# First group of a chunked recurrence: both scans first, score copies behind the packs, the turn behind those alone, 32 zero products ahead of the first T product

## The chip, the cores and the metric

One Trainium2 chip; the kernel runs on 1 core. The metric is the device time in microseconds of one execution. Engines: TensorE (PE, with its weight loads PEld), VectorE (DVE), ScalarE (ACT), GpSimd (POOL), SyncE (SP), and 16 DMA engines. Each engine works through its own instructions in the order in which they were put, and waits where an operand isn't ready. The order is made once, when the kernel is built: the program says what hangs on what, and a scheduler places the rest. Time before: 885.09 us, the median of three runs (878.41 to 887.28).

## What is computed

A recurrence over 768 steps for 4 x 8 heads with a 40 x 40 state, and behind it a layer of eight experts:

```python
for t in range(S):
    y[:, :, t] = np.einsum('bhd,bhde->bhe', rt, state)
    Sa = np.einsum('bhde,bhe->bhd', state, at)
    state_decay = state * wt[:, :, None, :] - np.einsum('bhd,bhe->bhde', Sa, bt)
    state = state_decay + np.einsum('bhd,bhe->bhde', vt, kt)
...
top2 = np.argpartition(-noisy_logits, 2, axis=1)[:, :2]
for e in range(E):
    for k in range(2):
        mask = top2[:, k] == e
        h = np.maximum(x[mask] @ w1[e], 0.0)
        out[mask] += top2_w[mask, k, None] * (h @ w2[e])
```

N is 3072 tokens, D 320, F 1024. The change lies in the recurrence alone.

## The kernel before

The 768 steps are cut into 12 chunks of 64 for each of two batch pairs p; `run` goes through the 24 chunks n = 0 to 23, p changing fastest. Two chunks of both pairs, four n, make a group g; there are six groups. For each group and pair some preparation is done ahead of its chunks:

- `prepA(G,raw)`: a scan over the decays w (the running product, `Gx`), its logarithm and the exponential of the negative on ACT (the inverse), three products for `NH` (a refined and shifted inverse) and `NG_`, then b times `NH` and a times `NG_`. `pack1` then splits b and a into a high and a low fp16 part: the high is a cast on ACT, the low a product on DVE, both in a buffer `pk` of which there are three (`PKB`). Three transfers for each, `st_ab<-pk`, stack them for PE: two need the high part alone, one the low.
- `prepC`: k times `NH`, packed as well, through DRAM (`d_k`) into `st_k`.
- `scoresL`: the score products `psc` of b and a for each chunk c, evicted from PSUM by DVE into `X` (the part for the solve) and by ACT into `lo`. PSUM has one buffer for them (`PPB`), so the products of the next chunk wait for both.
- `prepT`: `turn` transposes `X`, then `tsolve` inverts all 32 x 32 triangles in 30 steps of a product and an addition each; for group 0 on DVE, for the others on POOL (`TPOOL`). `prepU` turns `X` back: T is ready.

A chunk n is `pre` (the product `ak`, W), `chain` (T times W, twice, with a copy on ACT each time; the new state), `outp` and `blocks`. `warm(src,k)` issues k products of zeros into a PSUM tile that is overwritten later; `ND[0]` is 2.

The order around the change is set by the program's own sequence, by `V.run(z,at)`, which puts a preparation's DVE instructions behind the instruction `at` (a `Behind` object adds that edge and no wait), by `issue_after`, and for the rest by the scheduler. In `run`, the two preparations of group 0 stand one after the other, the score products are told to come behind the last cast `s.pa`, group 1's first preparation runs up to its b and a products with the k product of pair 1, and the turn of group 0 is put behind that k product by an edge of its own (`mk` behind `kl`). SP issues all transfers of this part.

## Time and profile before

| what | value |
|---|---|
| time, median of three | 885.09 us (878.41 to 887.28) |
| profiled execution | 874.69 us, of which the span 872.9 us |
| PE busy | 724.7 us (83%) |
| DVE busy | 593.7 us (68%) |
| ACT busy | 377.6 us (43%) |
| POOL busy | 366.1 us (42%) |
| DMA | 121.09 MB, mean 139 GB/s |

The span runs from the first to the last instruction; 1.8 us lie around it. Busy shares are means over stages that differ: the recurrence takes about the first half, the experts the second, and the work of this change lies in the first 100 us or so. What an edit is worth there is read from the waits and the order of time in that stretch, not from the table.

### The profile page before, as it was taken

Reading aid. Unit: us, or ns where it says so; the run is one execution under the profiler, and the core shown is the slowest. Engines: PE = TensorE matmul, PEld = TensorE weight load, DVE = VectorE, ACT = ScalarE, POOL = GpSimd, SP = SyncE. Lnnn points to the kernel's source line nnn. Section 1 sums busy time; section 2 is a strip of 40 time slices with the busy share of each in tenths; the row PEclk is TensorE's granted clock in tenths of the full one; section 3 lists DMA queues with packets and bytes.
Section 4 is the critical chain, followed back from the end, with each engine's and each line's share of the span. In section 5 each row is a group of like instructions: output and inputs, shape, how many; then the busy total and the mean of one; then the engine's idle time right before and its main releaser. Section 6 shows DMA issues by size and latency. Waiting matters only on the chain.

```text
span 872.9 us, 32590 instructions
## 1 busy us (share of the span) xinstructions
PE 724.7 (83%) x14248; PEld 647.4 (74%) x14248; DVE 593.7 (68%) x1305; ACT 377.6 (43%) x780; POOL 366.1 (42%) x512
## 2 busy tenths in 40 slices
PE   0124875899879787988998789999999999999993
PEld 0124664777767666777787688999999999999993
DVE  7799866887898897667667846828273746565530
ACT  3214444456555453544455525434343534444420
POOL 7000297495495396085002044344343434252222
PEclk9999889799999998999999999999999999999998
DMA  7766666477676284552223726594848585756312
GB/s 189 200 151 162 184 168 169 116 188 184 178 206 184 89 213 139 154 181 67 84 83 105 234 43 115 133 150 133 148 134 142 140 138 141 137 141 123 47 21 34
DMA packets 99508, 121.09 MB, mean 139 GB/s; under 512 B 37832, under 2 KB 83596, under 8 KB 99276
## 3 DMA queue, kind: packets, MB, share of 16 engines
q1 hardware_dynamic: 89244, 101.87, 45.3%
q0 software_dynamic: 10112, 17.05, 11.3%
q8 instruction: 113, 1.85, 0.9%
q14 instruction: 39, 0.32, 0.1%
HBM read 76.69 MB, written 24.74 MB: 116 GB/s over the span
## 4 chain that ended last, share of the span: by engine, by line
PE 62%; DVE 21%; POOL 5%; issue 4%; DMA 4%; ACT 3%; SPq 1%; POOLq 0%; DVEq 0%; ACTq 0%
PE ph L323 21%; PE po L350 18%; PE pW L563 4%; PE psc L563 4%; PE pY L563 3%; POOL X L686 3%; POOL Tt L684 2%; PE pQ L563 2%; DMA st_ab<-pk 2%; DVE pk L461 2%; PE pS L563 1%; DVE NH L461 1%; PE pst L563 1%; DVE P L807 1%; DVE X L461 1%
## 5 line engine op out<-in xcount | busy, mean ns | idle before, releaser
L353 POOL DMA_INDIRECT out_dram<-y,oi x56 | 87.5, 1563 | 188.0 <-ACT y L352 160.5
L323 PE MATMUL ph<-xT,w1h 128*128 128x256 f16 (+1 forms) x1280 | 137.3, 253 | 3.7 <-DVE xT L297 2.9
L323 PEld LDWEIGHTS <-w1h 128*128 128x128 f16 x1280 | 108.5, 98 | 12.3 <-issue 4.0
L350 PEld LDWEIGHTS <-hh 128*128 128x128 f16 x1536 | 107.9, 98 | 3.0 <-issue 3.0
L686 POOL TENSOR_TENSOR X<-X,Tt 128x30 f32<-128x30 f32 (+9 forms) x150 | 102.7, 685 | 11.1
L325 ACT ACTIVATE r<-ph 128x320 f32<-128x320 f32 (+1 forms) x128 | 65.3, 515 | 78.7 <-PE ph L323 63.5
L684 POOL TENSOR_TENSOR Tt<-X 128x30 f32<-128x30 f32 (+9 forms) x150 | 93.9, 626 | 10.7
L323 PE MATMUL ph<-xT,w1l 128*128 128x256 f16 (+1 forms) x768 | 89.4, 253 | 0.0
L261 DVE SCALAR_TENSOR_TENSOR w2l<-w2r,w2h 128x1280 f16<-128x1280 f32 x16 | 23.3, 1490 | 85.1 <-ACT w2h L260 85.1
L329 DVE TENSOR_TENSOR hl<-r,hh 128x256 f16<-128x256 f32 (+1 forms) x128 | 71.9, 562 | 4.0
L279 POOL DMA_INDIRECT xr<-xd,gi x56 | 57.4, 1025 | 34.5 <-ACT r L325 20.3
L679 POOL MEMSET X<- 128x32 f32 x5 | 0.8, 156 | 165.5 <-DVE X L676 165.5
L323 PEld LDWEIGHTS <-w1l 128*128 128x128 f16 x768 | 66.0, 98 | 4.4
L563 PEld LDWEIGHTS <-st_ab 120*32 120x32 f16 (+2 forms) x1312 | 26.7, 110 | 50.1 <-issue 47.7
L350 PE MATMUL po<-w2h,hh 128*128 128x160 f16 x768 | 61.1, 233 | 0.5 <-DVE f L153 0.5
L350 PE MATMUL po<-w2h,hl 128*128 128x160 f16 x768 | 61.0, 233 | 0.0
L350 PE MATMUL po<-w2l,hh 128*128 128x160 f16 x768 | 61.0, 233 | 0.0
L327 DVE CAST hh<-r 128x320 f16<-128x320 f32 (+1 forms) x128 | 49.1, 386 | 15.9 <-ACT r L325 15.6
L352 ACT ACTIVATE y<-po,tab 128x320 f32<-128x320 f32 x44 | 22.9, 521 | 77.9 <-PE po L350 77.9
L563 PE MATMUL psc<-RV,uT 128*64 128x128 f32 x384 | 54.3, 286 | 2.6 <-DVE P L807 2.4
L563 PE MATMUL pQ<-w,X 32*32 32x40 f32 x2304 | 39.6, 204 | 19.9 <-DVE X L676 7.5
L563 PEld LDWEIGHTS pQ<-w,X 32*32 32x32 f32 x2304 | 33.3, 111 | 29.8 <-issue 16.2
(352 smaller groups left out, 1601.9 us busy)
## 6 DMA issues: line engine op xcount, KB each, us to landing
st_ab<-pk SPq DMA_DIRECT2D x72, 180.0 KB
w2r<-in_w_dram SPq DMA_DIRECT2D x8, 1280.0 KB
RV<-in_rv_dram SPq DMA_DIRECT2D x48, 192.0 KB
w1r<-in_w_dram SPq DMA_DIRECT2D x8, 1024.0 KB
rawba<-in_fm_dram SPq DMA_DIRECT2D x20, 360.0 KB
raww<-in_fm_dram SPq DMA_DIRECT2D x12, 365.6 KB
d_k<-pk SPq DMA_DIRECT2D x12, 360.0 KB
st_k<-d_k SPq DMA_DIRECT2D x24, 180.0 KB
```

The costliest lines, as they stand in the source:

```text
L261: nc.vector.scalar_tensor_tensor(l,w,sc,o,op0=ALU.mult,op1=ALU.subtract,accum_out=s.wsum[:,s.nw:s.nw+1]); s.nw+=1
L279: k=t//128; s.held(nc.gpsimd.indirect_dma_start(out=X[:p,k if s.cap==CAP else 0],out_offset=None,in_=s.xd[int(w is not s.early[0])],in_off ...
L323: for a,b in cut(n): nc.tensor.matmul(ph[:,a:b],w[:,k,fs],X[:,j,t0+a:t0+b],start=i+a==0,stop=i==7,skip_group_check=True)
L325: g=nc.scalar.activation(r[:,:n],ph[:,:n],AF.Relu,scale=HSC/(XS*W1S))
L327: nc.vector.tensor_copy(hh[:,f,:n],r[:,:n])
L329: if c.stop>c.start: nc.vector.tensor_tensor(o,r[:,c],hh[:,f,c],op=ALU.subtract)
L350: for a,b in cut(DM): s.lm=nc.tensor.matmul(po[:p,a:b],h[:,f,r],w[:,f,a:b],start=k+a==0,stop=k==23,skip_group_check=True)
L353: st=nc.gpsimd.indirect_dma_start(out=s.out_d,out_offset=OFFS(ap=idx[:p,e,ii:ii+1],axis=0),in_=y[:p],in_offset=None,compute_op=ALU.add)
L461: i=f(*a,**k)
L563: def mm(s,*a,**k): return lambda: s.nc.tensor.matmul(*a,**k)
L684: eng.tensor_tensor(t,Xt[:,j:j+1,j+1:].to_broadcast([128,j,m]),Xt[:,0:j,j:j+1].to_broadcast([128,j,m]),op=ALU.mult)
L686: s.tl=eng.tensor_tensor(Xt[:,0:j,j+1:],Xt[:,0:j,j+1:],t,op=ALU.add)
```

## The change

`run` loads both decays ahead of everything else (`loadW`), and takes one step of each preparation in turn, so that both scans stand first; the second scan writes into a buffer of `st_ab` (`s3`), since `Gx` has one. The last pack's transfers are issued by ACT (`q`) and not by SP. DVE's copies of the first pair's scores are put behind the last low part (`pd`); the turn behind that alone, with its edge behind the k product gone; the k product of pair 1 behind step 20 of the solve (`tm0`). Chunk 0 gets 32 products of zeros (`NWU`) and not 2.

```diff
-NOUT=3072+896
+NOUT=3072+896; NWU=32
...
+    def loadW(s,p,g):
+        w=s.inp.tile([120,NS*65],F32,name="raww",bufs=2); s.nc.sync.dma_start(w,s.aps[0][p,g][:,:NS*65])
+        return w
-    def loadA(s,p,g,z=None):
+    def loadA(s,p,g,z=None,w=None):
...
-        w=s.inp.tile([120,W0],F32,name="raww",bufs=2); nc.sync.dma_start(w,FM[p,g][:,:W0])
+        if w is None: w=s.loadW(p,g)
...
-    def prepA(s,G,raw):
+    def prepA(s,G,raw,Gx=None,q=None):
...
-        Gx=s.tmp.tile([120,NS,65],F32,name="Gx")
+        if Gx is None: Gx=s.tmp.tile([120,NS,65],F32,name="Gx")
...
-        def stack(x):
+        def stack(x,e=nc.sync):
             def f(pk):
-                for q,l in ((40,0),(80,1),(0,x)): s.sd0=nc.sync.dma_start(sv[q:q+40,:,x],pk[:,l])
+                for q,l in ((40,0),(80,1),(0,x)): s.sd0=e.dma_start(sv[q:q+40,:,x],pk[:,l])
...
-        la=s.pack1(a_,-SC,0,1,stack(0))
+        la=s.pack1(a_,-SC,0,1,stack(0,q or nc.sync))
...
-    def scoresL(s,G,gi,scr):
+    def scoresL(s,G,gi,scr,f=None):
-        nc=s.nc
+        nc=s.nc; V=Behind(s.tc,nc.vector,f) if f is not None else nc.vector
...
-            s.sx=nc.vector.scalar_tensor_tensor(scr[:,q:q+8],pp[:,:,0:32],-(2.0**-18),s.tri.to_broadcast([128,8,32]),op0=ALU.mult,op1=ALU.mult)
+            s.sx=V.scalar_tensor_tensor(scr[:,q:q+8],pp[:,:,0:32],-(2.0**-18),s.tri.to_broadcast([128,8,32]),op0=ALU.mult,op1=ALU.mult)
...
-            s.warm(U,ND[0])
+            s.warm(U,ND[0] if o['n'] else NWU)
...
-        rA[0,0]=s.loadA(0,0)
+        w0=s.loadW(0,0); w1=s.loadW(1,0)
+        rA[0,0]=s.loadA(0,0,None,w0)
...
-        rA[0,1]=s.loadA(1,0,[xb(),xb()]); rC[0,0]=s.loadC({'p':0,'g':0})
+        rA[0,1]=s.loadA(1,0,[xb(),xb()],w1); rC[0,0]=s.loadC({'p':0,'g':0})
         s.consts1()
-        V.run(s.prepA(G_(0,0),rA[0,0])); rA[1,0]=s.loadA(0,1); V.run(s.prepA(G_(0,1),rA[0,1])); sd,pd=s.sd0.ins,s.pd
+        s3=s.sab[3].tile([120,18*K],F16,name="st_ab").bitcast(F32)[:,0:NS*65].rearrange("p (a b)->p a b",a=NS)
+        A=s.prepA(G_(0,0),rA[0,0]); B=s.prepA(G_(0,1),rA[0,1],s3,nc.scalar)
+        next(A); next(B); V.run(A); rA[1,0]=s.loadA(0,1); sd=s.sd0.ins; V.run(B); pd=s.pd
...
-            for p in range(2): scores(0,p)
+            for p in range(2): scores(0,p,None if p else pd)
...
-        prepT(0,s.pd); mk=s.xd; tl0=s.tl; tm0=s.tm
+        prepT(0,s.pd); tl0=s.tl; tm0=s.tm
...
-        for _ in range(5): next(z)
-        V.at=s.pl; c=s.prepC(grp[0][1],k1); next(c); kl=s.kl; V.at=tm0; next(c)
+        for _ in range(3): next(z)
+        V.run(s.prepC(grp[0][1],k1),tm0)
+        V.at=f1; next(z); next(z)
...
-        s.tc.add_manual_dep(mk.ins,kl.ins.name,mybir.DependencyInfo(mybir.DependencyClass.NoSync,mybir.DependencyReason.DATA),reason="behind")
```

The order on DVE at the start of the program, from the first scan on: `Gx` or, in the change, `st_ab` takes the scan, `raww` holds the inverse, `rawba` is b and a of pair 0. Before:

```order
L593 SCALAR_TENSOR_TENSOR Gx<-raww,d_111 120x780
L600 TENSOR_TENSOR NH<-Gx,raww 120x768
L603 SCALAR_TENSOR_TENSOR raww<-NH,raww 120x768
L605 TENSOR_TENSOR NH<-raww,Gx 120x768
L608 TENSOR_TENSOR NG__210<-Gx,raww 120x768
L613 TENSOR_TENSOR nge_212<-Gx,raww 120x12
L626 TENSOR_TENSOR rawba<-rawba,NH 120x768
L629 TENSOR_TENSOR rawba<-rawba,NG__210 120x768
L616 TENSOR_TENSOR gm<-nge_212,Gx 120x2x3x2
L553 SCALAR_TENSOR_TENSOR pk<-rawba,pk 120x768
L593 SCALAR_TENSOR_TENSOR Gx<-raww,d_111 120x780
L553 SCALAR_TENSOR_TENSOR pk<-rawba,pk 120x768
```

And in the change:

```order
L596 SCALAR_TENSOR_TENSOR Gx<-raww,d_111 120x780
L596 SCALAR_TENSOR_TENSOR st_ab<-raww,d_111 120x780
L603 TENSOR_TENSOR NH<-Gx,raww 120x768
L603 TENSOR_TENSOR NH<-st_ab,raww 120x768
L606 SCALAR_TENSOR_TENSOR raww<-NH,raww 120x768 x2
L608 TENSOR_TENSOR NH<-raww,Gx 120x768
L611 TENSOR_TENSOR NG__214<-Gx,raww 120x768
L616 TENSOR_TENSOR nge_216<-Gx,raww 120x12
L608 TENSOR_TENSOR NH<-raww,st_ab 120x768
L611 TENSOR_TENSOR NG__245<-st_ab,raww 120x768
L616 TENSOR_TENSOR nge_247<-st_ab,raww 120x12
L629 TENSOR_TENSOR rawba<-rawba,NH 120x768
```

Both scans now stand first, the two preparations alternate, and the low parts (`pk`) come behind all the products of both pairs.

The order on ACT in the same place, with buffer numbers and what each instruction waits for (DMAHW are the counters of transfers): lines 596/599 and 597/600 are the logarithm and the exponential, `pk` the casts, in the order b, a of pair 0, b, a of pair 1. Before:

```order
L596 ACTIVATE raww_177<-Gx_202 120x768 [waits DMAHW0_49,DVE_49]
L597 ACTIVATE raww_177<-raww_177 120x768 [waits Activation_49]
L551 ACTIVATE pk_219<-rawba_179 120x768 [waits DVE_49]
L551 ACTIVATE pk_222<-rawba_179 120x768 [waits DVE_49]
L596 ACTIVATE raww_184<-Gx_237 120x768 [waits DMAHW3_49,DVE_49]
L597 ACTIVATE raww_184<-raww_184 120x768 [waits Activation_49]
L551 ACTIVATE pk_254<-X_182 120x768 [waits DVE_49]
L551 ACTIVATE pk_257<-X_183 120x768 [waits DMAHW1_49,DMAHW2_49,DMAHW0_49,DVE_49]
```

And in the change:

```order
L599 ACTIVATE raww_177<-Gx_203 120x768 [waits DMAHW0_49,DVE_49]
L599 ACTIVATE raww_179<-st_ab_201 120x768 [waits DMAHW1_49,DVE_49]
L600 ACTIVATE raww_177<-raww_177 120x768 [waits Activation_49]
L600 ACTIVATE raww_179<-raww_179 120x768 [waits Activation_49]
L551 ACTIVATE pk_223<-rawba_181 120x768 [waits DVE_49]
L551 ACTIVATE pk_226<-rawba_181 120x768 [waits DVE_49]
L551 ACTIVATE pk_254<-X_184 120x768 [waits DVE_49]
L551 ACTIVATE pk_257<-X_185 120x768 [waits DMAHW1_49,DMAHW5_49,DMAHW0_49,DVE_49]
L626 DMA st_ab_252<-pk_257 40x3x768 [waits DMAHW2_49,Activation_49]
L626 DMA st_ab_252<-pk_257 40x3x768 [waits DMAHW4_49]
L626 DMA st_ab_252<-pk_257 40x3x768 [waits DMAHW6_49,DVE_49]
L673 ACTIVATE lo_269<-psc_270 128x256 [waits DVE_49]
```

Both logarithms stand ahead of both exponentials, and behind the fourth cast ACT issues that pack's three transfers, with the eviction and k's cast behind them. The fourth cast waits for three transfers of earlier packs in both orders.

The order on DVE around the second turn (`X<-X` of 32x32, group 1's), where chunk 0 ends and chunk 1 runs: `ak` belongs to `pre` of chunk 2, `uT` to the output of chunk 1, `rawk` is k of group 1's second pair. Before, from the copy `vu` on:

```order
L785 TENSOR_SCALAR vu<-pQ 64x320
L671 SCALAR_TENSOR_TENSOR X<-psc,tri 128x256
L102 SCALAR_TENSOR_TENSOR xT<-px,xT 128x384
L794 SCALAR_TENSOR_TENSOR Sst_162<-pS,gam_138 128x8x40
L461 TENSOR_TENSOR rawba<-rawba,NG__977 120x768
L671 SCALAR_TENSOR_TENSOR X<-psc,tri 128x256
L750 TENSOR_TENSOR sfs<-Sst_162,sfs 128x320
L676 STREAM_TRANSPOSE X<-X 128x32x32
L725 TENSOR_TENSOR ak<-psc,mk_123 128x512
L461 SCALAR_TENSOR_TENSOR pk<-rawba,pk 120x768
L567 COPY uT<-pu 128x512
L461 SCALAR_TENSOR_TENSOR pk<-rawba,pk 120x768
```

And in the change, from the state of chunk 1 on:

```order
L797 SCALAR_TENSOR_TENSOR Sst_162<-pS,gam_138 128x8x40
L461 TENSOR_TENSOR rawba<-rawba,NG__1007 120x768
L728 TENSOR_TENSOR ak<-psc,mk_123 128x512
L461 SCALAR_TENSOR_TENSOR pk<-rawba,pk 120x768
L753 TENSOR_TENSOR sfs<-Sst_162,sfs 128x320
L674 SCALAR_TENSOR_TENSOR X<-psc,tri 128x256
L102 SCALAR_TENSOR_TENSOR xT<-px,xT 128x384
L567 COPY uT<-pu 128x512
L461 SCALAR_TENSOR_TENSOR pk<-rawba,pk 120x768
L461 TENSOR_TENSOR rawk<-rawk,NH 120x6x64 x2
L674 SCALAR_TENSOR_TENSOR X<-psc,tri 128x256
L679 STREAM_TRANSPOSE X<-X 128x32x32
```

`ak`, two low parts (`pk`), `uT` and the k products (`rawk`, two instructions) stood behind the turn and now stand ahead of it. POOL's order is the same in both, and PE's differs in the first four chunks.

## Rows read from the trace of the kernel before

**Rows 1.** Waits, 135 to 175 us; columns: who for whom, us in total, times, longest

```profile
PE pQ L563 <- DVE X L461: 5.4, 1, 5.4
DVE X L461 <- POOL X L686: 4.6, 1, 4.6
```

**Rows 2.** Timeline, POOL, start of group 1's solve; columns: start us, us, instruction, [idle before]

```profile
104.08 0.15 POOL L679 MEMSET X<- 128x32 f32 x1 [85.55 <-DVE X L676]
```

**Rows 3.** Waits of DVE in the first 69 us

```profile
DVE X L671 <- PE psc L563: 5.4, 2, 3.4
DVE NH L600 <- ACT raww L597: 2.7, 2, 1.8
DVE pk L461 <- ACT pk L551: 0.5, 1, 0.5
```

**Rows 4.** Timeline, DVE, the first pair's preparation

```profile
4.90 1.78 DVE L593 TENSOR_TENSOR_SCAN Gx<-raww,d 120x780 f32<-120x780 f32 x1 [1.01 <-DMA raww<-in_fm_dram]
8.47 0.96 DVE L600 TENSOR_TENSOR NH<-Gx,raww 120x768 f32<-120x768 f32 x1 [1.78 <-ACT raww L597]
9.46 0.96 DVE L603 SCALAR_TENSOR_TENSOR raww<-NH,raww 120x768 f32<-120x768 f32 x1
12.40 0.95 DVE L626 TENSOR_TENSOR rawba<-rawba,NH 120x768 f32<-120x768 f32 x1
13.27 0.97 DVE L629 TENSOR_TENSOR rawba<-rawba,NG__210 120x768 f32<-120x768 f32 x1
```

**Rows 5.** Timeline, SP's queue; then the chain of work, start us, us, what

```profile
14.25 5.18 SPq L623 DMA_DIRECT2D st_ab<-pk  x6
...
18.68 5.00 DMA st_ab<-pk
65.02 2.44 DMA st_k<-d_k
```

**Rows 6.** Timeline, PE; sums of two windows: PE, PEld, DVE, ACT, POOL busy (instructions), PEclk, ...

```profile
61.03 0.71 PE L710 MATMUL pQ<-dm,idh 128*128 128x320 f16 x2
61.54 0.47 PE L563 MATMUL pS<-dm,idh 128*128 128x320 f16 x1
...
69.54 1.29 PE L563 MATMUL pQ<-w,X 32*32 32x40 f32 x64 [7.53 <-DVE X L676]
...
90.46 0.79 PE L563 MATMUL pQ<-w,X 32*32 32x40 f32 x64
...
69.50:70.80 1.30, 1.26 (x64) 1.16 (x64) 1.30 (x2) 0.56 (x1) 0.00 (x0) 1.00 0.05 13
151.80:153.20 1.40, 1.34 (x65) 1.25 (x65) 1.40 (x4) 0.00 (x0) 0.00 (x0) 0.50 0.14 38
```

**Rows 7.** Timeline, DVE and then POOL behind the second turn, and POOL at the solve's end

```profile
103.84 0.66 DVE L725 TENSOR_TENSOR ak<-psc,mk 128x512 f32<-128x512 f32 x1
104.41 0.96 DVE L461 SCALAR_TENSOR_TENSOR pk<-rawba,pk 120x768 f16<-120x768 f32 x1
105.28 0.69 DVE L567 COPY uT<-pu 128x512 f32<-128x512 f32 x1
105.88 0.96 DVE L461 SCALAR_TENSOR_TENSOR pk<-rawba,pk 120x768 f16<-120x768 f32 x1
106.74 1.03 DVE L461 TENSOR_TENSOR rawk<-rawk,NH 120x384 f32<-120x384 f32 x2
...
104.48 0.98 POOL L686 TENSOR_TENSOR X<-X,Tt 128x30 f32<-128x30 f32 x1
...
105.91 2.01 POOL L686 TENSOR_TENSOR X<-X,Tt 128x58 f32<-128x58 f32 x1
...
148.80 0.31 POOL L686 TENSOR_TENSOR X<-X,Tt 128x58 f32<-128x58 f32 x1
...
149.52 0.26 POOL L686 TENSOR_TENSOR X<-X,Tt 128x30 f32<-128x30 f32 x1
```

**Rows 8.** Sum of the window between the two turns; columns as in rows 6

```profile
69.24:101.90 32.66, 22.99 (x634) 19.05 (x635) 29.51 (x48) 17.99 (x34) 0.00 (x0) 1.00 0.69 184
```

More of the change, by code (lines that the diff above doesn't have):

```diff
@@ L825, in G_, with scores @@
             grp[g].append({'p':p,'g':g}); return grp[g][p]
-        def scores(g,p): s.scoresL(grp[g][p],p,scr[g])
+        def scores(g,p,f=None): s.scoresL(grp[g][p],p,scr[g],f)
         E=lambda g: nc.gpsimd if g in TPOOL else nc.vector
```

## The prediction

> **What bounds the kernel now.** The 40 slices of the page show TensorE (PE) at nine tenths or more in the last third, and a mixed picture in the first 150 us; that is where the change lies, so I read that stretch by waits, then by the timeline, and only at the end by sums over a window. The waits around 150 us give the key: VectorE (DVE) waits 4.6 us for GpSimd's (POOL's) last addition, and PE waits 5.4 us behind it for the turned T matrices of group 1 [rows 1]. The chunks 1 to 3 are done by then, chunk 4 can't begin. So the end of POOL's solve of group 1 sets the time, and that solve begins when DVE's turn of X is done, at 104.08 us [rows 2]. Ahead of it DVE is the engine that is seldom idle: it does the first group's packs, group 0's own solve, and group 1's packs. What counts is therefore when DVE reaches the second turn. What comes earlier there can give back at most 4.6 us, since DVE and PE then stand ready; what comes later costs its full length, because everything from chunk 4 on hangs on it.
>
> **DVE up to the end of group 0's solve.** Before, DVE waits here for causes that the change attacks: 2.7 us in two waits for ScalarE's (ACT's) logarithm and exponential, 5.4 us in two waits for score products behind the stack transfers, and 0.5 us for a cast [rows 3]: 8.6 us together. The work in this stretch is the same before and after (the two k products only move into the solve), so the difference of the idle time decides. I walk through the new order:
>
> - Both scans come first, 4.90 us and 1.78 us later [rows 4]; the second `raww` is now second in the load queue. ACT has both logarithms ahead of both exponentials, so the first exponential waits for the second scan. Before, logarithm and exponential filled the 1.78 us between the scan's end and NH [rows 4], 0.9 each. Now the two scans end near 8.4, and the second logarithm and the first exponential follow until 10.2: DVE idles 1.8 us, as much as before in the first of its two waits. Only the other, 0.9, is gone.
> - The two preparations are interleaved. A dependent instruction starts 0.99 us after the one it needs (8.47 to 9.46), an independent one 0.87 us after its neighbour (12.40 to 13.27) [rows 4]. Some four dependent pairs are parted: 4 x 0.12 = 0.5 us gained.
> - The b product of pair 0 stood 3.93 us behind the first NH (8.47 to 12.40). Now four large instructions of the other pair are in between, 3.5 us, and a few dependent gaps fewer: it starts near 17.4, is cast by 19.25 (an activation of this shape being 0.9), and the last of the three low parts that need no wait (pair 1's b) ends near 23.8 (seven large instructions at 0.87, and small ones).
> - The fourth pack is the catch. `pk` has three buffers (PKB), and the fourth reuses the first's. ACT's cast into it waits for all three transfers of pair 0's b. Before, they were the first three of a run of six that SP began at 14.25 [rows 5], ten microseconds ahead of it. Now b's third is the sixth in SyncE's (SP's) queue. The six took 5.18 us, 0.86 each: it goes out at 19.25 + 5 x 0.86 = 23.6. From issue to landing the last of that burst took 5.00 us, and the shortest transfer of the chain, one out of d_k with little beside it, 2.44 us [rows 5]. This one is in mid-burst, so I take the middle, 3.7: landed at 27.3, cast by 28.2. DVE, in order, stands from 23.8 to 28.2: 4.4 us, with bounds 3.1 and 5.7. Behind it in DVE's queue stand k's products, the score evictions and group 1's scan, so all of them come later.
> - ACT then issues that pack's three transfers itself. No such issue is in the trace; between nothing and SP's 0.86 each I take the latter, the nearest row. Behind them wait the score's eviction and k's cast, and DVE waits for that cast, 1.3 us by this walk (0 if the issue costs nothing).
> - The turn needs `f` (the packs) alone now, but the scan and the two activations of group 1's first pair stand ahead of it as before. Their wait was hidden in the 3.4 us for the score product [rows 3]; bare, it is 1.8 us.
>
> New idle time: 1.8 + 4.4 + 1.3 + 1.8 = 9.3 us against 8.6; less the 0.5 of the interleaving, group 0's solve ends 0.2 us later. With the bounds of the landing, -1.1 to +1.5. The stall has moved from the score products to the pack buffer.
>
> **The 32 zero products.** Before, two of them started at 61.03, and pS behind them at 61.54 [rows 6]: 0.25 each, 32 in 8.2 us. They begin behind pW as the two did and end near 69.3, just inside the 7.53 us that PE waits for the turned X until 69.54 [rows 6]; they cost nothing there. If that cover is gone, they cost their overhang, under 1 us. What they may give is the clock. The first T product takes 1.29 us, its like at 90.46 0.79 [rows 6]. At 151.8, after 5.4 us of idling, the same 1.3 us goes with a granted clock of 0.50, the lower level of 1.2 GHz; for 69.5 the view prints 1.00 [rows 6], but the length is that of the lower level, and I go by it. So chunk 0 runs at the lower level, and each of its four bursts might gain 0.5 us. I count nothing: q's copy stands behind a pack's cast on ACT, the next copy behind a logarithm, so ACT's order and not PE sets the pace, and the pack work on DVE that leads to the second turn doesn't wait for chunk 0.
>
> The Trainium skill ("TensorE: Matmul & The Clock Gate", Part 1: The HAM clock gate) says that sustained activity lifts the gate and an idle stretch puts it back. By that rule chunk 0 starts at the higher level, since the products end shortly before the T product, and the sum would be up to 2.0 us lower; the rows of before show the lift only behind a busy stretch (90.46), and no row shows what chunk 0's own gaps do to it.
>
> **From group 0's solve to the second turn.** Here the order shows the other cost. Six instructions that stood behind the second turn now stand ahead of it: ak 0.66, a low part 0.96, uT 0.69, another low part 0.96, k's two products 1.03 [rows 7]: 4.3 us. Against it, DVE was busy 29.51 us of the 32.66 between the first turn and the second, idle 3.15 [rows 8]. Some of that is filled, since chunk 1's score products no longer stand first in PE's queue ahead of `pre`. None to all of it; I take 1.0, since the waits for ACT (an exponential, an eviction) stay. The second turn comes 0.2 + 4.3 - 1.0 = 3.5 us later.
>
> **What the solve gives back.** Right behind the turn POOL's second and fourth additions took 0.98 and 2.01 us, while DVE ran the two low parts and k's products; the additions of the same sizes at the solve's end, with DVE waiting for it, took 0.26 and 0.31 [rows 7]. That is 0.72 + 1.70 = 2.4 us lost to those very instructions, which now run before the solve. I take all of it; the other bound is nothing, if the next pack work meets POOL in their place.
>
> **Sum.** 0.2 + 3.3 - 2.4 = +1.1 us for chunk 4's start, and from there the order is nearly that of before. The profiled execution took 874.69 us (span 872.9 and 1.8 around it), so it would take 875.8. It is the fastest of the four executions shown; against the median of 885.09 the same 1.1 us gives 886.2. The bounds: best -1.1 + 4.3 - 3.15 - 2.4 = -2.4; worst 1.5 + 4.3 - 0 - 0 = +5.8.
>
> **Rivals.**
>
> 1. *POOL's relief does not come.* Place: the first microseconds behind the second turn. DVE's next pack work (a low part, k's other products) follows there directly now, and the solve loses the same 2.4 us to it. The turn's 3.5 us then come through whole: 888.6. For it: the same kinds of instruction do stand there. Against it: three instructions fewer meet the solve in all. It decides if the solve stays at 45.7 us (104.08 to 149.78) with a start later than that.
> 2. *The clock holds.* The zero products carry chunk 0 at the higher level and its chain, not ACT's queue, sets when state and `ak` are ready. 1.1 - 2.0 = -0.9, and with DVE's 3.15 us of waits gone too, -3.0: 882. Against it: the copies' places on ACT. The rule of the Trainium skill quoted above ("TensorE: Matmul & The Clock Gate", Part 1) speaks for it.
> 3. *The pack buffer costs little.* b's third transfer lands as the lone one did, in 2.44 us, and ACT's issues cost nothing: -1.3 - 1.3 + 1.1 = -1.5: 883.6. Against it: eight more transfers are in the queues then.
> 4. *The change doesn't do what it says.* Scans first gives no shorter wait, as shown; that is in the forecast.
>
> **How the numbers follow.** Forecast, near no change, 0.57; rival 1 0.2; rival 2 0.13; rival 3 0.1. The predicted time is the forecast's, 886.2. The rivals reach from 882 to 891; the median itself is of runs between 878.41 and 887.28, half of which (4.4) I add at the lower end, and half of that above: 878 to 893. A measurement of this kernel can tell about 1%, 8.9 us, from no change. No case reaches that: the most that the wait can give is 4.6, the worst sum 5.8. What lies outside comes from the spread of the runs: faster 0.1, same 0.82, slower 0.08.
>
> **What would show it.** DVE's wait for the fourth pack's cast, 3 to 6 us near 24 us; no wait of 3.4 us for a score product; group 0's first T product within 1.5 us of 69.54; the second group's turn near 105; POOL's solve near 43 us instead of 45.7, and DVE's wait at its end. I am wrong if the fourth cast doesn't wait, if the second turn comes before 102, or if the time moves while POOL's solve ends where it did.

## The result: 0.7% slower, and where the first 160 us went

| | before | after |
|---|---|---|
| median of 20 runs, us | 883.86 (878.38 to 890.02) | 890.07 (884.11 to 897.37) |
| ratio, 95% interval | | 1.0071 [1.0044, 1.0097] |
| profiled execution, us (span) | 874.69 (872.9) | 891.90 (890.1) |

The change costs about 6 us. The two profiled executions lie 17 us apart because that of before is faster than every other run of it, and that of after a little over its median; so stages are compared here, and a second profile of each kernel (below) stands beside the first.

| start, us | before | after | difference | forecast |
|---|---|---|---|---|
| group 0's turn | 41.96 | 45.61 | +3.7 | |
| group 0's turn back (solve done) | 67.38 | 71.80 | +4.4 | +0.2 |
| group 1's turn | 101.90 | 110.43 | +8.5 | +3.5 |
| length of POOL's solve | 45.70 | 43.48 | -2.2 | -2.4 |
| group 1's turn back | 149.82 | 156.14 | +6.3 | +1.1 |

The waits of DVE in the first 70 us of after (who for whom, us in total, times, longest), which answer to [rows 3]:

```profile
DVE pk L553 <- ACT pk L551: 5.4, 1, 5.4
DVE X L674 <- PE psc L563: 3.3, 1, 3.3
DVE NH L603 <- ACT raww L600: 1.6, 1, 1.6
DVE NH L461 <- ACT raww L600: 1.5, 1, 1.5
DVE pk L461 <- ACT pk L551: 1.2, 1, 1.2
```

With a sixth of 0.6, again for a score product, these are 13.6 us; before they were 8.6, and the forecast said 9.3. Four of the waits are the forecast's own. The second is not: DVE still waits for a score product. The timeline of DVE in after has both, and the four turns (start us, us, instruction, [idle before and what ended it]):

```profile
28.83 0.96 DVE L553 SCALAR_TENSOR_TENSOR pk<-X,pk 120x768 f16<-120x768 f32 x1 [5.36 <-ACT pk L551]
...
42.00 0.42 DVE L674 SCALAR_TENSOR_TENSOR X<-psc,tri 128x256 f32<-128x256 f32 x1 [3.35 <-PE psc L563]
...
45.61 2.04 DVE L461 STREAM_TRANSPOSE X<-X 128x1024 f32<-128x1024 f32 x1
...
71.80 2.00 DVE L679 STREAM_TRANSPOSE X<-X 128x1024 f32<-128x1024 f32 x1
...
110.43 2.06 DVE L679 STREAM_TRANSPOSE X<-X 128x1024 f32<-128x1024 f32 x1
...
156.14 2.02 DVE L461 STREAM_TRANSPOSE X<-X 128x1024 f32<-128x1024 f32 x1 [3.00 <-POOL X L689]
```

The chain of work of after through this stretch (start us, us, what) shows what stood ahead of the score product:

```profile
23.40 4.45 DMA st_ab<-pk
27.96 0.85 ACT pk L551
28.83 9.05 DMA st_ab<-pk
```

The sixth transfer lands at 27.85 and frees the pack buffer, as forecast (4.45 us, where 3.7 was taken and 5.00 was the upper bound, [rows 5]). Then the fourth pack's transfers need 9 to 10 us each. The last of the three, issued at 31.15, landed at 41.20 by the counts of its semaphore, 10.05 us later, and the third score product could start only then, at 41.34 (before: 36.00). What stood ahead of it is in the timeline of SP's and ACT's queues; the last two rows are the third score product on PE, in after and in before:

```profile
18.98 6.03 SPq L626 DMA_DIRECT2D st_ab<-pk  x7
25.06 1.34 SPq L588 DMA_DIRECT2D rawba<-in_fm_dram  x2
26.51 1.59 SPq L626 DMA_DIRECT2D st_ab<-pk  x2
28.14 0.61 SPq L651 DMA_DIRECT2D st_ab<-in_fm_dram  x1
...
28.83 3.11 ACTq L626 DMA_DIRECT2D st_ab<-pk  x3
...
41.34 0.62 PE L563 MATMUL psc<-st_ab 120*32 120x64 f16 x32 [8.30 <-DMA RV<-in_rv_dram]
```

```profile
36.00 0.62 PE L563 MATMUL psc<-st_ab 120*32 120x64 f16 x32 [7.34 <-DMA st_ab<-pk]
```

In after the profile names a load of RV as what ended PE's wait. That load counts on a semaphore that the pack's first transfer had used, the product doesn't read it, and it was not complete until 41.83; so I go by the pack's last landing, 0.14 us ahead of the product. So ahead of ACT's first transfer stood three loads of 360 KB and nine stack transfers of 180 KB, issued within ten microseconds. Before, the twelve stack transfers ran as two bursts of six, from 14.25 and from 26.74 us, with two loads between them.

Group 1's solve: sums of POOL's window in before, in after, and in an experiment, before_32 (columns as in [rows 6]: PE, PEld, DVE, ACT, POOL busy with instructions, then PEclk, DMA share, GB/s):

```profile
104.08:149.78 45.70, 33.34 (x868) 27.82 (x868) 30.08 (x42) 19.90 (x44) 41.08 (x61) 0.90 0.63 165
```

```profile
112.62:156.10 43.48, 31.73 (x756) 26.98 (x756) 26.42 (x36) 18.94 (x44) 38.85 (x61) 0.80 0.62 158
```

```profile
108.81:154.62 45.81, 32.42 (x795) 27.32 (x795) 30.27 (x40) 21.60 (x47) 41.18 (x61) 0.82 0.63 170
```

POOL does the same 61 instructions each time. With DVE 3.7 us less busy beside it (six instructions fewer) they take 2.2 us less; with DVE as busy as before, nothing is saved.

### The profile page after: what moved, and what is told of

Read it like the earlier page. It is cut to its first block, busy times and chain, and to the rows that moved or that the text cites. A ratio compares the mean times of both kernels' runs of the same rounds, so it can differ in the third digit from the quotient of the medians.

```text
span 890.1 us, 32644 instructions
## 1 busy us (share of the span) xinstructions
PE 738.9 (83%) x14278; PEld 658.5 (74%) x14278; DVE 593.1 (67%) x1305; ACT 377.4 (42%) x780; POOL 364.6 (41%) x512
## 4 chain that ended last, share of the span: by engine, by line
PE 48%; DVE 19%; issue 13%; POOL 10%; DMA 5%; ACT 3%; SPq 0%; POOLq 0%; DVEq 0%; ACTq 0%
PE ph L323 13%; PE po L350 13%; PE pW L563 4%; PE psc L563 4%; PE pY L563 3%; POOL out_dram L353 3%; POOL xr L279 2%; POOL X L689 2%; POOL Tt L687 2%; DMA st_ab<-pk 2%; PE pQ L563 2%; PE pS L563 2%; DVE pk L461 1%; DVE Gx L461 1%; PE pst L563 1%
## 5 line engine op out<-in xcount | busy, mean ns | idle before, releaser
L689 POOL TENSOR_TENSOR X<-X,Tt 128x30 f32<-128x30 f32 (+9 forms) x150 | 98.3, 655 | 11.1
L687 POOL TENSOR_TENSOR Tt<-X 128x30 f32<-128x30 f32 (+9 forms) x150 | 97.7, 651 | 10.7
L325 ACT ACTIVATE r<-ph 128x320 f32<-128x320 f32 (+1 forms) x128 | 65.2, 515 | 84.5 <-PE ph L323 63.9
L329 DVE TENSOR_TENSOR hl<-r,hh 128x256 f16<-128x256 f32 (+1 forms) x128 | 71.8, 562 | 4.0
L563 PEld LDWEIGHTS <-st_ab 120*32 120x32 f16 (+2 forms) x1312 | 25.4, 107 | 53.9 <-issue 43.9
L563 PE MATMUL psc<-RV 128*64 128x128 f32 x384 | 54.1, 283 | 1.6 <-issue 1.6
L350 PEld LDWEIGHTS <-hl 128*128 128x128 f16 x768 | 55.3, 99 | 0.0
```

The source lines that it names most:

```text
L325: g=nc.scalar.activation(r[:,:n],ph[:,:n],AF.Relu,scale=HSC/(XS*W1S))
L329: if c.stop>c.start: nc.vector.tensor_tensor(o,r[:,c],hh[:,f,c],op=ALU.subtract)
L350: for a,b in cut(DM): s.lm=nc.tensor.matmul(po[:p,a:b],h[:,f,r],w[:,f,a:b],start=k+a==0,stop=k==23,skip_group_check=True)
L563: def mm(s,*a,**k): return lambda: s.nc.tensor.matmul(*a,**k)
L687: eng.tensor_tensor(t,Xt[:,j:j+1,j+1:].to_broadcast([128,j,m]),Xt[:,0:j,j:j+1].to_broadcast([128,j,m]),op=ALU.mult)
L689: s.tl=eng.tensor_tensor(Xt[:,0:j,j+1:],Xt[:,0:j,j+1:],t,op=ALU.add)
```

## The experiments

Turns in us, "back" is the turn back when a solve is done; all from one profile each. Ratios are to the kernel before on the same chip, with their intervals.

| kernel | group 0's turn | back | group 1's turn | POOL's solve | back | last turn | ratio |
|---|---|---|---|---|---|---|---|
| before | 41.96 | 67.4 | 101.9 | 45.7 | 149.8 | 424.8 | |
| before_again | 42.32 | 67.7 | 102.7 | 45.4 | 150.3 | 422.6 | 0.9987 [0.9941, 1.0033] |
| after | 45.61 | 71.8 | 110.4 | 43.5 | 156.1 | 433.7 | 1.0071 [1.0044, 1.0097] |
| after_again | 44.56 | 70.7 | 108.8 | 43.8 | 154.8 | 428.1 | 1.0107 [1.0052, 1.0161] |
| late_loads | 42.84 | 69.0 | 107.0 | 46.2 | 155.5 | 428.0 | 1.0060 [1.0022, 1.0097] |
| own_buffer | 42.86 | 69.0 | 108.8 | 45.8 | 156.8 | 429.3 | 1.0055 [1.0027, 1.0083] |
| turn_first | 45.00 | 71.1 | 108.5 | 45.4 | 156.1 | 429.9 | 1.0097 [1.0066, 1.0127] |
| two_zeros | 44.59 | 70.7 | 105.5 | 45.8 | 153.5 | 429.9 | 1.0079 [1.0050, 1.0108] |
| three_undone | 44.08 | 70.2 | 105.1 | 45.4 | 152.8 | 426.8 | 1.0077 [1.0047, 1.0107] |
| before_32 | 41.97 | 67.3 | 106.7 | 45.8 | 154.7 | 429.9 | 1.0044 [1.0007, 1.0080] |
| one_after_other | 37.46 | 65.2 | 99.7 | 45.7 | 147.6 | 423.1 | 0.9994 [0.9964, 1.0025] |
| sp_queue | 42.58 | 68.8 | 104.1 | 45.4 | 151.7 | 422.5 | 1.0025 [0.9989, 1.0061] |
| room_for_packs | 38.51 | 64.7 | 99.2 | 45.5 | 146.8 | 420.0 | 0.9972 [0.9943, 1.0001] |
| copies_behind | 41.19 | 66.6 | 101.7 | 45.9 | 149.8 | 421.0 | 0.9991 [0.9962, 1.0020] |

Two profiles of the same kernel differ by up to 1.1 us at the first turn, 1.6 at group 1's turn and 5.6 at the last. Early differences of 2 us and more are therefore read from single profiles; what reaches the end is read from the ratios.

**late_loads: the loads that stand ahead of the fourth pack**

```
- next(A); next(B); V.run(A); rA[1,0]=s.loadA(0,1); sd=...; V.run(B); pd=s.pd
+ next(A); next(B); V.run(A); w2=s.loadW(0,1); sd=...; V.run(B); pd=s.pd
...
  f1=s.pd
+ with after(f1.ins): rA[1,0]=s.loadA(0,1,None,w2)
```

> The changed kernel, with the two 360 KB loads of group 1's first rawba (SP, 25.06 and 25.64 us after) issued behind chunk 0's fetches instead of behind pair 0's stacks; nothing else moved. Landing theory (the fourth pack's three transfers land 9 to 10 us after their issue because these loads stand ahead of them): the 5.4 us wait for the fourth pack's cast at 24 us stays, the three transfers land 4 to 6 us after issue, the 3.35 us wait at 42.00 for the score product shrinks to under 1 us, the first turn starts near 42.3 us instead of 45.61, and the whole is 2 to 3 us shorter than the changed kernel (about 1.004 of the kernel before, where the changed kernel is 1.007). Buffer theory (the wait for the pack buffer alone makes the turn late): first turn within 1 us of 45.6, ratio 1.007. Order theory (the loss lies in the second segment): first turn anywhere, second turn still 110, ratio 1.007.

The chain of this kernel has, for the fourth pack's last transfer:

```profile
30.64 7.79 DMA st_ab<-pk
```

7.8 us instead of 10.05 (31.15 to 41.20; 8.85 in after_again): the loads were part of it, but the k load and chunk 0's fetches behind it moved up and took their place. The wait for the score product is down to 1.1 us and group 0's turn starts at 42.84, as the landing theory said (1.7 us ahead of after_again, 2.8 ahead of after). The landing of 4 to 6 us was too hopeful. Group 1's turn is still at 107.0: the second loss is another one. The ratio, 1.0060, can't be told from that of the changed kernel.

**own_buffer: a fourth pack that waits for no buffer**

```
-        pk=s.tmp.tile([120,nc_*2,X//nc_],F16,name="pk",bufs=PKB)
+        if pk is None: pk=s.tmp.tile([120,nc_*2,X//nc_],F16,name="pk",bufs=PKB)
...
+ p4=s.sab[2].tile([120,18*K],F16,name="st_ab")[:,0:2*X]...
```

> The changed kernel, with the fourth pack in memory of its own (a part of a stack that is not used yet) instead of the first of three pack buffers, so that its cast waits for no transfer. Buffer theory: the 5.4 us wait near 24 us is gone, the fourth pack's transfers are issued from about 24.5 us on instead of 28.83, stand ahead of the loads or between them and land near 33 to 35 us; the last score product then waits for whichever of b's and a's stacks of pair 1 lands last (b's landed at 35.26 us); the first turn starts at 38.5 to 40.5 us instead of 45.61, which is ahead of the 41.96 of the kernel before; the whole 4 to 6 us shorter than the changed kernel, ratio 1.000 to 1.003. Landing theory alone (the loads decide, not the buffer): the wait moves to the score product, first turn within 2 us of 45.6. Order theory: second turn within 2 us of 110, ratio 1.007.

The stall moved by one pack. The rows are of ACT and of DVE in this kernel's timeline:

```profile
31.25 0.84 ACT L551 ACTIVATE pk<-rawk 120x768 f16<-120x768 f32 x1 [9.61 <-DMA st_ab<-st_ab]
...
32.13 0.96 DVE L461 SCALAR_TENSOR_TENSOR pk<-rawk,pk 120x768 f16<-120x768 f32 x1 [6.67 <-ACT pk L551]
```

k's pack now asks for the buffer that the fourth pack gave up, and the transfer that frees it (the sixth on SP) lands at 31.15 instead of 27.85, since ACT's three transfers now run beside it. (The profile names ACT's own transfers as the releaser; those landed at 26.7, 29.0 and 31.6, the sixth on SP 0.1 us ahead of the cast.) DVE, in order, stands 6.7 us. The first turn gains 2.7 us (1.7 against after_again), not 5 to 7.

**sp_queue: the fourth pack's transfers on SP, and 2 zero products**

```
- B=s.prepA(G_(0,1),rA[0,1],s3,nc.scalar)
+ B=s.prepA(G_(0,1),rA[0,1],s3)
...
- NWU=32
+ NWU=2
```

> The changed kernel with the fourth pack's three transfers issued by SP again instead of ACT, and 2 zero products; the scans stay interleaved. Landing theory (the twelve transfers and two loads are served in turn, whoever issues them): the fourth pack's transfers stand on SP behind b's stacks, land at 38 to 41.5 us as in two_zeros, first turn at 43.5 to 45.6 us, ratio as two_zeros, 1.006 to 1.010. ACT theory (three issues of 0.8 to 1.4 us on ACT ahead of the k cast and the lo copies make the turn late): k's cast 3 us earlier, first turn 2 to 3 us earlier, ratio 1.003 to 1.005.

Beside two_zeros (44.59), which issues them on ACT, the turn is 2.0 us earlier; the last transfer is issued at 30.07 and takes 8.09 us. So a share of the loss was ACT's: its three issues took 3.11 us (the ACTq row of after above), the first of them 1.39 and the others 0.79 each, where SP's took 0.75 to 0.98; the last left at 31.15 in after and 30.83 in two_zeros. The Trainium skill ("DMA: Bandwidth & Descriptors", Issuing engines are not separate DMA queues) says that another issuing engine saves only the time of issuing, since all transfers run on the same DMA engines. The runs agree that no second path opened: in two_zeros the first transfer that ACT issued, at 28.50, landed at 37.65, behind the last of SP's stack transfers (34.95). The last one took 9.35 us there and 8.09 on SP; the k load of 360 KB stands ahead of it in two_zeros and behind it here, so this difference is not the issuing engine's alone.

**one_after_other: the interleaving taken out, the score copies and the turn left as changed, 2 zero products**

```
...
- A=s.prepA(...); B=s.prepA(...,s3,nc.scalar)
- next(A); next(B); V.run(A); rA[1,0]=s.loadA(0,1); sd=s.sd0.ins; V.run(B); pd=s.pd
+ V.run(s.prepA(G_(0,0),rA[0,0])); rA[1,0]=s.loadA(0,1); V.run(s.prepA(G_(0,1),rA[0,1])); sd,pd=s.sd0.ins,s.pd
```

> The changed kernel with the two preparations one after the other again (loads, scans and SP queue as in the kernel before) and 2 zero products; what stays of the change: pair 0's score products behind pair 1's packs, the turn behind those, k's packs in one piece. If the interleaving is what makes the first turn late: pair 0's six stack transfers leave SP from 14.3 us again instead of 19, pair 1's from 24.5 instead of 26.74 (DVE no longer waits 1.95 us for the first score product ahead of them), its last lands near 33.7 instead of 35.86, the first turn starts at 37 to 39.5 us (41.96 before, 44.6 to 45.6 changed), group 1's turn 3 to 4.5 us ahead of the kernel before, ratio 0.993 to 0.998. If the score products behind the packs are the cause: first turn at 43 or later, ratio over 1.003. Third way: the turns come ahead but the end doesn't move, ratio 0.999 to 1.002.

Group 0's turn starts at 37.46, 4.5 us ahead of before and 7 to 8 ahead of after: the rest of the change does what it says, and the late turn comes from the interleaving with all that hangs on it. Half of the gain is lost at once: two of group 1's products of 0.92 and 0.95 us, and smaller ones, now stand behind the turn, ahead of the solve's first step; from the turn to the turn back it takes 27.8 us instead of 25.4. What is left, 2.1 us at the turn back and 2.2 at group 1's turn (3 to 4.5 were expected), can't be seen in the ratio.

**three_undone: own buffer, late loads and 2 zero products together**

> The changed kernel with the fourth pack in memory of its own, group 1's two rawba loads behind chunk 0's fetches, and 2 zero products instead of 32: the two causes found in the first pair, and the second segment's order, taken out together; the interleaved scans and the turn behind the packs stay. If the losses are these three and add: the k pack's cast, which waited 6.7 us for its buffer in own_buffer, waits under 4; the first turn starts at 37 to 39.5 us (41.96 in the kernel before); from group 0's turn back to group 1's turn it takes 34.5 to 35.5 us as in two_zeros, so group 1's turn starts at 97.5 to 100.5; POOL's solve takes 45 to 46; the later turns lie 2 to 4 us ahead of the kernel before, ratio 0.994 to 0.998. Rival (the scans' order itself loses elsewhere, or the first group's time is not what sets the end): turns ahead as said, but the ratio stays at 1.000 to 1.006. Second rival (late loads are missed): group 1's first products near 65 to 75 us wait for rawba.

This missed: the turn came at 44.08. The rows of DVE, then of PE, tell why:

```profile
30.79 0.96 DVE L461 SCALAR_TENSOR_TENSOR pk<-rawk,pk 120x768 f16<-120x768 f32 x1 [5.60 <-DMA st_ab<-pk]
...
43.62 0.42 DVE L674 SCALAR_TENSOR_TENSOR X<-psc,tri 128x256 f32<-128x256 f32 x1 [3.60 <-PE psc L563]
...
41.41 0.64 PE L563 MATMUL psc<-st_ab,st_k 120*64 120x64 f16 x16 [3.54 <-DMA st_k<-d_k]
...
42.94 0.62 PE L563 MATMUL psc<-st_ab 120*32 120x64 f16 x32
```

k's pack still waits 5.6 us for its buffer, and in this order PE has chunk 0's `ak` product, which needs k's stack from DRAM, ahead of the fourth score product. So undoing both causes of the first pair's lateness gained less than undoing either alone (42.8 and 42.9): one pack still waits, what stands behind it follows, and PE's order changed as well.

**room_for_packs: the same, with k's pack in its own memory too and all twelve transfers on SP**

```
...
- V.run(s.prepC(grp[0][0],rC[0,0]),pd)
+ V.run(s.prepC(grp[0][0],rC[0,0],t2[:,2*X:4*X]...),pd)
...
- B=s.prepA(G_(0,1),rA[0,1],s3,nc.scalar,p4)
+ B=s.prepA(G_(0,1),rA[0,1],s3,None,p4)
```

> The changed kernel with scans still interleaved, but the fourth pack and k's pack each in memory of their own, all twelve stack transfers on SP, group 1's two loads behind chunk 0's fetches, and 2 zero products. If it was the missing pack buffers and the mixed queues, not the interleaving, that made the first turn late: no wait for a pack near 24 us, the twelve transfers leave SP one after the other from 18.7 to 29 us, the last lands at 32.5 to 34.5, the first turn starts at 37 to 39.5 us (44.6 to 45.6 changed, 42 before). If the interleaving itself is late (it starts pair 0's transfers 4.7 us later, and twelve of them need 15 us on the DMA engines): last landing at 36 or later, first turn at 40.5 or later. Ratio: if a gain in the first turn is passed on whole, 0.994 to 0.997; if half of it is lost in group 0's solve and behind, as in one_after_other, 0.998 to 1.001.

Its timeline, SP's queue and then DVE:

```profile
18.83 7.68 SPq L626 DMA_DIRECT2D st_ab<-pk  x9
26.61 2.42 SPq L626 DMA_DIRECT2D st_ab<-st_ab  x3
...
38.51 2.06 DVE L461 STREAM_TRANSPOSE X<-X 128x1024 f32<-128x1024 f32 x1
```

Twelve transfers in one run; the last, issued at 28.27, lands at 33.41 after 5.15 us, and the turn is at 38.51. So the interleaved scans are not late in themselves: with room for five packs, one queue, the loads behind and 2 zero products the same order of scans is 3.5 us ahead of before, and the solve, turn and chunk stages pass it on (99.2 against 101.9 and 102.7 at group 1's turn, 420.0 against 424.8 and 422.6 at the last). It is the fastest kernel of the study: 0.9972 of before, with an interval that just reaches 1, and 1.0 to 1.3% under the changed kernel by the two ratios of that one. Which part of it is the buffers, which the one queue and which the late loads was not told apart further. Nor is the gain the interleaving's: one_after_other, without it and without the extra buffers, has its first turn at 37.46 and its turn back at 65.2 (64.7 here). What both share of the change is that the copies of the scores stand behind the packs, the turn behind those alone, and the k product of pair 1 in the solve.

**two_zeros: 2 zero products instead of 32**

> The changed kernel with 2 zero products ahead of chunk 0's first T products instead of 32. Theory of the prediction (they lie in TensorE's wait and buy nothing): chunk 0 takes the same time within 0.5 us, second turn at 110 to 111, ratio within 0.002 of the changed kernel's 1.007, although the granted clock of the stretch behind them falls towards 0.5 where the changed kernel has 1.00. Clock rival: without them the products of chunk 0 and of the scores behind it run at half the clock and the second turn comes 1.5 to 2.5 us later. Opposite rival (the zero products themselves hold up chunk 0): second turn earlier by 1 to 3 us.

Group 1's turn comes at 105.48, and the way there from group 0's turn back takes 34.8 us, where after took 38.6 and after_again 38.1, before 34.5 and before_again 35.0. That is the opposite rival, with a little more than its 1 to 3 us: the zero products themselves bring the second loss. They do not do it by their time. In after's timeline of PE they are hidden as forecast:

```profile
64.64 5.87 PE L713 MATMUL pQ<-dm,idh 128*128 128x320 f16 x32
70.35 0.30 PE L563 MATMUL pS<-dm,idh 128*128 128x320 f16 x1
73.94 1.06 PE L563 MATMUL pQ<-w,X 32*32 32x40 f32 x64 [3.29 <-DVE X L679]
```

They do it by the order. With this one number as the only edit the order of PE, DVE, ACT and SP comes out otherwise from chunk 0 on; only POOL's stays. That the scheduler counts the 32 products as work of PE when it places the rest is my reading; no run shows its accounts. DVE's rows around group 1's turn (TURN), with 2 products (-) and with 32 (+), shortened:

```
- xt<-pY,xt   vu<-pQ   X<-psc   xT<-px   Sst   rawba<-rawba,NG__   X<-psc   sfs   TURN   ak   pk   uT   pk   rawk
+ vu<-pQ   xt<-pY,xt   Sst   rawba<-rawba,NG__   ak   pk   sfs   X<-psc   xT<-px   uT   pk   rawk   X<-psc   TURN
```

These are the six instructions of the prediction's second term. They moved because of the 32 products, not because of the scans. Most of the lead goes again in the solve: with the six instructions behind the turn POOL takes 45.8 us, and not 43.5 and 43.8, so of 3.3 to 5.0 us at group 1's turn 1.4 to 2.7 are left at its turn back. The ratio, 1.0079, shows none of it.

**before_32: the kernel before with 32 zero products**

```
- s.warm(U,ND[0])
+ s.warm(U,ND[0] if o['n'] else 32)
```

> The kernel before with one edit: 32 zero products instead of 2 ahead of chunk 0's first T products. If the second segment's loss comes from the zero products (through the order in which the program is laid out, which moves six DVE instructions and the chunk's work ahead of group 1's scores as in the changed kernel): first turn at 42, group 0's turn back at 67.4, group 1's turn at 105 to 107 instead of 101.9, POOL's solve 43 to 44 us instead of 45.7, ratio 1.000 to 1.005. If it came from the interleaved scans or the split of prepC: group 1's turn within 1 us of 101.9. Clock rival: the products behind run at the full clock and the turn comes 1 to 2 us earlier, ratio 0.997 to 0.999. The two outcomes in the ratio tell how much of the 6 us the zero products alone carry.

This is the clean proof of it: group 0's turn and turn back stand where they were, group 1's turn comes at 106.65, 39.3 us behind the turn back instead of 34.5, and the kernel is slower by 0.44% [0.07, 0.80]. PE's timeline in this kernel:

```profile
60.98 5.34 PE L710 MATMUL pQ<-dm,idh 128*128 128x320 f16 x32
66.15 0.30 PE L563 MATMUL pS<-dm,idh 128*128 128x320 f16 x1
69.46 1.29 PE L563 MATMUL pQ<-w,X 32*32 32x40 f32 x64 [3.01 <-DVE X L676]
...
93.72 0.81 PE L642 MATMUL pg<-gm,selg 120*64 120x6 f32 x12 [1.48 <-ACT lo L670]
94.47 1.27 PE L563 MATMUL pQ<-w,X 32*32 32x40 f32 x32
95.67 1.94 PE L563 MATMUL pY<-kb,P 128*64 128x64 f32 x32
```

In the new order the gammas `pg` wait for a score copy that DVE and ACT reach late, chunk 1's second T product stands behind them, and the products that follow go at the lower level: pY, a product of a chunk's output, takes 1.94 us, where before took 1.13:

```profile
94.72 1.13 PE L563 MATMUL pY<-kb,P 128*64 128x64 f32 x32
```

So on the path to group 1's turn there are DVE's six instructions, that wait, and products at half the clock. What each of the three is worth no run takes apart, except for four of the instructions in turn_first. POOL's solve was not shorter here (45.81): other DVE work, 30.27 us in all, took the place of the six instructions. That part of the expectation was wrong.

**turn_first: four DVE instructions put behind group 1's turn again, with 32 zero products**

```
- V.tick(slots['S'],s.aD)
+ V.tick(slots['S'],s.xd if n==1 else s.aD)
...
- with after(s.aP.ins) if n<2 else ExitStack(): s.pre(O[n+1])
+ with after(s.aP.ins) if n<2 else ExitStack(): s.pre(O[n+1],s.xd if n==1 else None)
```

> The changed kernel, with DVE's rawba product, ak of chunk 2 and two packs put behind group 1's turn instead of ahead of it (0.95 + 0.68 + 2 x 0.95 = 3.5 us; the uT copy and two k products of 0.68 + 1.0 us still stand ahead). Order theory: the first turn is unchanged at 45.6 us, group 1's turn starts at 106.5 to 108 us instead of 110.43, POOL's solve starts that much earlier, still takes 43 to 44 us, and the whole is 2.5 to 3.5 us shorter than the changed kernel, ratio about 1.004. Rival: the four instructions ahead of the turn stood in idle time of DVE (it waits there for xt's transposed gammas and the score product anyway), the turn moves by under 1 us and the ratio stays at 1.007. Second rival: the moved four come late for chunk 2 and for group 2's stacks and give the gain back there: turn at 107, but the next turns of the changed kernel (222.7, 232.8) within 1 us of where they were.

Group 1's turn comes at 108.54, a little behind the 106.5 to 108 expected, and the ratio, 1.0097, shows no gain. The way to group 1's turn takes 37.4 us instead of 38.6 and 38.1, so 0.7 to 1.2 us of the 3.5 come back. Most of the four stood in time in which DVE had to wait for the score product anyway, which supports the reading that PE's order and clock carry much of the second loss, without showing it. POOL's relief went with them (45.4).

**copies_behind: the kernel before with pair 0's score copies behind pair 1's packs, nothing else**

```
- for p in range(2): scores(0,p)
+ for p in range(2): scores(0,p,None if p else pd)
...
```

> The kernel before with one part of the change alone: pair 0's two score products on DVE stand behind pair 1's two packs. DVE's 1.95 us wait at 24.55 us goes, pair 1's transfers leave 2.3 us earlier, their last lands near 33.6 instead of 35.86; the first turn keeps its place behind NH, NG and k's products, so it starts at 39 to 40.5 us instead of 42, and group 0's solve keeps its 25.4 us: turn back at 64.5 to 66 as in one_after_other (65.2), by another way. Ratio if that gain reaches the end: 0.996 to 0.999; if the end does not follow the first group: 1.000 within 0.003.

The transfers leave 2.5 us earlier and the last lands at 33.81, as said, but the turn gains only 0.8 us. DVE's row in this kernel:

```profile
36.22 0.96 DVE L461 TENSOR_TENSOR NH<-Gx,raww 120x768 f32<-120x768 f32 x1 [1.18 <-ACT raww L597]
```

NH, the products behind it and k's products still stand ahead of the turn. No difference in time.

**after_again and before_again: second profiles**

> The changed kernel itself, unaltered, on the chip of the experiments, for a second profile and a ratio beside theirs. First turn at 45 to 46 us, group 1's turn at 109.5 to 111, ratio 1.004 to 1.010. Question: from the start of the last turn back to the end it took 456 us in the first profile of the changed kernel and 448 in that of the kernel before. If that belongs to the change, it takes 455 or more again; if it is the spread between executions, 448 to 454.

> The kernel before itself, for a second profile. First turn at 41.5 to 42.5 us, group 1's turn at 101.5 to 102.5, POOL's solve 45 to 46.5. From the start of the last turn back to the end: 447 to 450 if that stretch is steady and shorter in this kernel, 450 to 455 if it is spread.

The stages repeat within 1.6 us up to group 1's turn back, though after_again comes earlier than expected (44.56 and 108.80), and the loss at 155 us is 4.5 us here against 6.3. From the last turn to the end the four profiles take 448.2 and 452.8 (before), 456.4 and 455.3 (after). By the bound for after_again, 455, that would belong to the change; by the bound for before_again, 450 to 455, it is spread. The other kernels took 450.1 to 458.0 there. The 458.0 are one_after_other's, on a chip where the kernel before has a median of 885.93 us and not 874.88 as on that of the two second profiles, so it says little; on the latter chip after takes 2.5 us longer than before in this stretch, behind a last turn that is 5.5 us later. Whether any of the 2.5 us belongs to the change stays open.

## Why the prediction was right in the number and wrong in two of its steps

Predicted 886.2 (878 to 893), measured 890.07; within 1% was given 0.82, and it was 0.71%. The number lies in the range, but two terms were missed or put down to the wrong edit. That it lies there is partly luck: the sum said +0.1%, the measured +0.71% is clear of zero, and at group 1's turn back the loss of 6.3 us (4.5 in the second pair) stands at or over the worst sum, +5.8. The range was built out to that worst sum, 890.9 (the prediction counts it among the rivals), and 2.2 us beyond it; on the median of the twenty runs (883.86, and not 885.09) the worst sum gives 889.7, which 890.07 is just over.

**The solve of group 0, +0.2: wrong.** It was +4.4, and 3.0 in the second pair of profiles. Most items of the walk held: the fourth cast's wait 4.4 forecast, 5.36 measured; the logarithm and exponential 1.8 and 1.8, measured 1.6 and 1.5; k's cast 1.3, measured 1.2. What failed is the step that set the 5.4 us of waits for score products to nothing ("The stall has moved from the score products to the pack buffer"). It had moved to the buffer and stayed at the products too: 3.35 us and another 0.6. These 3.9 us and the 1.0 that the fourth cast took over its forecast, less 0.6 in the other waits, are the 4.3 us between 13.6 and 9.3. The walk followed the fourth pack up to its issue and gave no landing to the three transfers behind it. By [rows 5] the last transfer of a burst of six took 5.00 us; here, behind eleven others and three loads, the last took 10.05 (8.85 in after_again). The runs name the pieces: without two of the loads ahead 7.8 us, on SP 8.1, with room for all packs, one queue and no load ahead 5.15, and the turn earlier each time.

**Six DVE instructions ahead of group 1's turn, +3.3: right in size, wrong in cause.** Measured +4.1 in the first pair of profiles and 3.1 in the second. The prediction read the order rightly but put it beside the scans, and gave the 32 zero products no cost. two_zeros and before_32 show that they alone make this order. The size agrees partly by luck: four of the six instructions gave back 0.7 to 1.2 of their 3.5 us when they were put behind the turn again, so much of the loss is carried by what else the new order brings, PE's wait for the gammas and its products at the lower level, and these the prediction did not have. To price the edit as work on PE was right (5.87 us, hidden; 8.2 forecast); to miss that it is also a number in the planning of the order was the error.

**The clock.** Counted as nothing, and nearly that: the first T product took 1.06 us instead of 1.29 in after, but 1.29 in after_again, before_32 and turn_first, which have the 32 products too. After that the clock didn't hold. Sums of after's windows behind the first T product, and around pY:

```profile
76.00:80.00 4.00, 2.42 (x64) 2.09 (x62) 3.94 (x6) 2.70 (x5) 0.00 (x0) 0.50 0.44 128
98.00:104.00 6.00, 6.00 (x136) 5.41 (x136) 3.25 (x8) 2.31 (x6) 0.00 (x0) 0.51 0.63 156
```

0.50 is the level of 1.2 GHz, after 3.29 us of waiting ahead of the first T product and more between the bursts. The zero products had lifted it: `pS` right behind them took 0.30 us, where it took 0.47 behind two [rows 6]. The rule of the Trainium skill ("TensorE: Matmul & The Clock Gate", Part 1) holds in both its directions here: the busy stretch of zero products lifted the clock, and chunk 0's waits put it back. What it would have given, up to 2.0 us, was 0.23 us in one profile of four. Rival 2 is out.

**POOL's relief, -2.4: measured -2.2 and -1.6.** As a whole rival 1 didn't come true in the changed kernel, but of the two additions that [rows 7] show (second and fourth instruction of the solve, and not second and fourth addition) it holds for the first. POOL's rows in after:

```profile
113.02 0.97 POOL L689 TENSOR_TENSOR X<-X,Tt 128x30 f32<-128x30 f32 x1
...
114.44 0.28 POOL L689 TENSOR_TENSOR X<-X,Tt 128x58 f32<-128x58 f32 x1
```

The first still takes 0.97 us (0.98 before), beside DVE's next low part; the second fell from 2.01 to 0.28. So 1.7 us came from where the prediction looked for 2.4, and the other 0.5 is the balance of longer and shorter instructions later in the solve: the size is again closer than the account. before_32 shows rival 1's mechanism over the whole solve: there DVE filled it again, and it took 45.81.

**The sum.** +1.1 forecast, +6.3 and +4.5 measured at group 1's turn back; the ratios, 1.0071 and 1.0107, are 6 to 9 us. The first pair's lateness and the zero products each cost 3 to 5 us at their stage; by the ratios two_zeros (the zero products undone, the late turn left) stays at 1.0079 and before_32 (the other way round) at 1.0044. The intervals are too wide to say whether the two add up. At group 1's turn back, by single profiles, two_zeros is 3.7 us behind before, before_32 4.8 and after 6.3; the 2.2 us missing from the sum are POOL's relief, which neither of the first two has (45.8 us each). What two_zeros still leads by there, 1.4 us against after_again, is gone by the last turn (429.9 against 428.1), and why was not settled.

Of the named signs, the wait near 24 us and POOL's 43 us came as said; the T product within 1.5 us of 69.54 (73.94), no wait for a score product (3.35) and the turn near 105 (110.43) did not. The first two misses point to the same step.

## What to carry to other kernels

Follow a moved transfer to its landing, not to its issue: give it the queue that stands ahead of it at its new time, on all issuing engines, and take the lag from a row with the same crowd. Work that is added into an idle stretch still counts in the planning of the order; build the edit alone and look at the order of every engine behind it before calling it free. A reordering that brings work together needs buffers for all of it at once: with five pack places, one queue and the loads out of the way the same order of scans came 3.5 us early, with three places and two queues 2 to 4 us late. And ask what the reordering itself adds: with the two preparations one after the other the rest of the change came 4.5 us early without any new buffer.

## What the runs showed of the hardware that was not expected

- The lag of a 180 KB stack transfer from issue to landing went from 3.3 us (the first of a burst) to 5.0 at the end of six in before and 5.15 at the end of twelve in room_for_packs, and to 10.05 in after (8.85 in after_again) with three 360 KB loads and eleven others issued in the 12 us before it.
- The first of three issues took ACT 1.39 us and the next two 0.79 each; SP's took 0.98 for the first of a burst and 0.75 to 0.77 for those right behind it, and one left every 0.86 us.
- The granted clock reads 1.00 early in a profile whatever the products' length, as if there were no record of it yet: in before the window at 69.5 us reads 1.00 while the T product has the length of the lower level [rows 6]. In after, where the zero products lifted it, 76 to 80 us reads 0.50 with the same length of product, 1.27 us. A mean of the column over early windows can't be compared between the two kernels.
- POOL's 61 instructions of a solve took 38.9 us beside 26.4 us of DVE work (after), 41.1 beside 30.1 (before) and 41.2 beside 30.3 (before_32).
